# Decay load on 32 partitions, score operands padded to 128 rows, and fewer fill steps in two batches of an attention and mixer kernel

## The chip, the cores and the metric

The kernel runs on one core of one Trainium2 chip. The metric is the device time in microseconds (us), the median of several executions. A profile's *span* (first to last instruction of one profiled execution) is about 1.8 us shorter than that execution's time in the two main profiles; I compare spans with spans and times with times. The engines are PE (tensor engine; PEld is its weight load), DVE (VectorE), ACT (ScalarE), POOL (GpSimd) and SP (SyncE, which issues transfers).

## The reference

```python
# q, k, v: (8 batches, 8 heads, 576, 64); s: (8, 8, 576)
scores = scale * q @ k.T                       # scale = 1/8
cum    = cumsum(max(s, 0))                     # along the sequence
bias   = min(-(cum[:, None] - cum[None, :]), 0)
attn   = softmax(where(causal, -1e9, scores + bias))
x      = (attn @ v) with the heads side by side     # (8, 576, 512)
u      = x + (x.T @ U @ V).T                   # low rank, along the sequence
out    = u + max(u @ w_ch1, 0) @ w_ch2         # 512 -> 2048 -> 512
```

## The kernel before

Attention and the mixer run interleaved on PE. Attention works on 32 pairs of heads, four pairs a batch. The mixer works on nine groups of 512 tokens, 32 *fill steps* a group (16 of `w_ch1`, 16 of `w_ch2`, four matmuls of 512 columns each). A string of tokens fixes the order: `D`/`E` are score products of a head (diagonal blocks, blocks below), `d f m l` their exponentials on ACT, `A` the product with v, `a` its division on DVE, `U X Y` the low-rank part, `T` a PE transpose of q and k (batches 0 and 1), `G` their transpose on DVE (later batches), `R` the fetch of decay rows, `L` the later decays, `Z` fills, `p` warming matmuls without use, `F` one fill step, `r` what follows it on ACT or DVE.

```python
def load_decays(i, s_sb):                # 32 rows of s, four times over: 128 partitions
    nc.sync.dma_start(out=s_sb, in_=bass.AP(..., i * FR * S, [[0, 4], [S, FR], [1, S]]))

def decays(rows, s_sb, cum):
    blk = [ds(i * FR, FR) for i in range(4)]                 # FR = 32
    nc.vector.tensor_scalar(s_sb, s_sb, 0.0, 1.0 / scale, op0=ALU.max, op1=ALU.mult)
    nc.vector.tensor_tensor_scan(cum, s_sb, s_sb, 0.0, op0=ALU.add, op1=ALU.max)
    nc.scalar.mul(rows[blk[3], 0, :], cum[blk[3]], -1.0)
    nc.scalar.copy(rows[blk[0], 1, :], upper(cum)[blk[0]])
    ...                                                      # two more pieces on DVE

def product(h, dst, j, lo, hi, start, stop):
    bias = bias_0 if h < 2 else None
    rows = D if bias else KA             # 64, or 64 + 4 rows of decays = 68
    nc.tensor.matmul(dst, lhsT=head_of(h)[0:rows, ds(S + j * 128, 128)],
                     rhs=head_of(h)[0:rows, lo:hi], ...)
    if bias:                             # heads 0 and 1: decays as a second product
        nc.tensor.matmul(dst, lhsT=bias[0][:, ds(j * 128, 128)], rhs=bias[1 + h][:, lo:hi], ...)

def play(tokens, pair=None):             # cut
    ...
        if kind == "G":
            n = pair // 2 + i            # group of four heads whose q and k are turned
    ...
            if kind == "y" and n % PB == PB - 1:       # a batch is done: queue its mixer group
                queue(n // PB)
                queue(100 + n // PB)

SEQ = ("p8 T0 tA0 tV0 T1 tA1 tV1 p8 | Z0 D0 d0 T2 tV2 tV2 E0 f0 m0 D1 d1 T3 tV3 tV3 E1 ... "
       "... Y7 yV7 Q1 Q101 F r F r F r F r F r F r F r L1 ")
PAIR = ("D0 d0 U-2 uV-2 X-2 F r E0 k0 f0 G1 m0 F r D1 d1 Y-2 yV-2 F r E1 k1 f1 G1 m1 l0 F r "
        "A-2 K0 a-2 F r A-1 a-1 F r F r F r ")     # from batch 2 on, once a pair
```

The softmax here doesn't subtract the row's maximum and nothing guards it: scores larger than these inputs give would overflow.

## Time and profile before

| | before |
|---|---|
| time, first three runs | 411.49 us (410.84 to 414.21) |
| span of the profile | 410.0 us |
| PE busy | 388.7 us, 95% |
| first score product | 13.98 us |
| first mixer matmul | 45.74 us |
| half clock | 17.17 to 34.24 and 140.05 to 146.88 us |

PE is the bottleneck, so what counts is where it waits and where its clock is low. From the profile's page: the busy table, then the span in 40 slices of 10.25 us; a digit is the busy share, or the granted PE clock, in tenths (9 is 90% or more).

```profile
PE 388.7 (95%) x3358; PEld 222.5 (54%) x3358; DVE 208.2 (51%) x439; ACT 199.1 (49%) x386; POOL 107.4 (26%) x173
...
PE   5999888989999799999999999999999999999996
...
PEclk9858999999999889999999999999999999999999
```

Three places stand out: the first slice is half idle; in slices 2 and 3 PE is "busy" but the clock is at 0.8 and 0.5; at slice 13 PE is at 0.7 and right after it the clock drops again. (The clock records begin with the first change, here at 13.76 us; the time before it is counted as full, though the warming matmuls there start 427 ns apart, which is half clock. The rows "half clock" of my tables begin with the first record too.)

The start, in the chain of waits in order of time (start us, us, what):

```profile
0.80 7.26 DMA hT<-in_s_dram
8.06 0.02 issue
8.09 0.47 DVE hT L185
...
8.58 1.37 DVE hT L186
...
12.11 0.99 DVE hT L601 x2
...
13.13 0.81 DVE slot L220
...
13.98 0.23 PE pscore L250
```

The load of s takes until 8.06 us, the decay operations another 5 us, and only then can DVE copy the first q and k for the first score product.

The hole near slice 13, in PE's timeline (start us, us, engine, line, operation, out<-in; in brackets idle time before it and what ended it):

```profile
133.80 0.81 PE L431 MATMUL pwork<-w_sb,hT 128*128 128x512 bf16 x3
...
137.42 0.42 PE L250 MATMUL pscore<-slot 68*128 68x128 bf16 x5
140.30 0.69 PE L359 MATMUL pwork<-x_sb,U_sb 128*128 128x128 bf16 x5 [2.46 <-DVE x_sb L345]
...
143.10 1.89 PE L414 MATMUL pwork<-uT,w_sb 128*128 128x512 bf16 x4
```

L431 and L414 are the two mixer products. Between 134.5 and 143.10 us there is none, PE waits 2.46 us for a division on DVE, and the four mixer matmuls at 143.10 then take 1.89 us.

### The profile page before, as it was taken

The page shows a single profiled execution, that of the slowest core. Times are in us where ns is not written, and L with a number is a line of the kernel's source. Part 1 is how long each engine was busy: PE and PEld are TensorE (multiplying, and loading weights), DVE is VectorE, ACT ScalarE, POOL GpSimd, SP SyncE. Part 2 cuts the span into 40 slices and gives each one's busy share as a digit, 9 for nine tenths or more (in the row PEclk, how much of TensorE's full clock was granted, in tenths as well). Part 3 has the DMA queues.
Part 4 walks back from the last instruction along what each step waited for, and adds up shares of the span by engine and source line. Part 5 has one row for each costly group of instructions (what it writes and reads, how often), then busy time and mean ns, then how long its engine had stood idle before and what let it go on. Part 6 is the DMA issues. An engine that isn't in the chain of part 4 may idle for free.

```text
span 410.0 us, 8377 instructions
## 1 busy us (share of the span) xinstructions
PE 388.7 (95%) x3358; PEld 222.5 (54%) x3358; DVE 208.2 (51%) x439; ACT 199.1 (49%) x386; POOL 107.4 (26%) x173
## 2 busy tenths in 40 slices
PE   5999888989999799999999999999999999999996
PEld 2367545645555555565556555555555555444442
DVE  4647654578466745665566556655665333102011
ACT  1466487406843557436743674367436730630610
POOL 8871458144304440624052406200000000000000
PEclk9858999999999889999999999999999999999999
DMA  8999999359454961696269625921222001001002
GB/s 124 178 201 154 179 106 127 43 96 212 76 92 92 158 100 30 106 149 108 41 103 153 104 44 96 159 60 32 58 82 57 2 26 53 26 27 55 23 26 77
DMA packets 76294, 37.23 MB, mean 91 GB/s; under 512 B 60616, under 2 KB 67816, under 8 KB 76256
## 3 DMA queue, kind: packets, MB, share of 16 engines
q0 software_dynamic: 65584, 18.43, 51.5%
q1 hardware_dynamic: 10672, 18.28, 15.6%
q8 instruction: 26, 0.43, 0.5%
q14 instruction: 12, 0.10, 0.1%
HBM read 37.95 MB, written 10.03 MB: 117 GB/s over the span
## 4 chain that ended last, share of the span: by engine, by line
PE 85%; DVE 8%; DMA 3%; ACT 2%; POOL 1%; issue 1%; DVEq 0%
PE pwork L414 29%; PE pwork L431 28%; PE pscore L250 11%; PE pwork L329 6%; PE pwork L359 2%; PE pwork L443 2%; DMA hT<-in_s_dram 2%; PE pwork L377 2%; DVE turned L234 2%; PE pwork L397 1%; DVE o_sb L454 1%; DVE uT L404 1%; DVE x_sb L345 1%; PE pscore L259 1%; PE pwork L208 1%; DMA v_slot<-in_v_dram 1%
## 5 line engine op out<-in xcount | busy, mean ns | idle before, releaser
L315 ACT ACTIVATE pT<-pscore 128x512 bf16<-128x512 f32 (+1 forms) x224 | 112.4, 558 | 85.9 <-PE pscore L250 74.2
L414 PE MATMUL pwork<-uT,w_sb 128*128 128x512 bf16 x576 | 140.8, 382 | 1.3 <-DVE uT L404 1.3
L431 PE MATMUL pwork<-w_sb,hT 128*128 128x512 bf16 x576 | 140.4, 379 | 0.0
L421 ACT ACTIVATE hT<-pwork 128x512 bf16<-128x512 f32 x144 | 86.4, 602 | 74.8 <-PE pwork L414 74.0
L414 PEld LDWEIGHTS <-w_sb 128*128 128x128 bf16 x576 | 52.4, 98 | 52.1 <-issue 2.1
L431 PEld LDWEIGHTS <-hT 128*128 128x128 bf16 x576 | 51.7, 98 | 47.9
L250 PE MATMUL pscore<-slot 68*128 68x128 bf16 (+5 forms) x576 | 72.6, 250 | 2.8 <-ACT pT L315 1.9
L250 PEld LDWEIGHTS <-slot 68*128 68x128 bf16 (+1 forms) x576 | 45.2, 101 | 37.6 <-issue 8.5
L454 DVE COPY o_sb<-pwork 128x512 f32<-128x512 f32 x36 | 24.9, 692 | 70.9 <-PE pwork L443 70.9
L126 POOL DMA_DIRECT2D qk_sd<-in_q_dram x48 | 27.1, 575 | 125.6 <-DVE turned L234 109.1
L234 DVE STREAM_TRANSPOSE turned<-qk_sd 128x576 bf16<-128x576 bf16 x48 | 54.5, 1138 | 0.7
L329 PEld LDWEIGHTS <-pT 128*128 128x128 bf16 x960 | 38.3, 99 | 14.5 <-issue 2.0
L318 DVE TENSOR_TENSOR pT<-pT,keep 128x512 bf16<-128x512 bf16 (+1 forms) x84 | 29.8, 355 | 28.2 <-ACT pT L315 27.3
L329 PE MATMUL pwork<-v_slot,pT 128*128 128x65 bf16 x960 | 40.6, 196 | 1.5 <-ACT slot L220 1.2
L370 DVE CAST ux<-pwork 128x128 bf16<-128x128 f32 x30 | 8.7, 290 | 48.1 <-PE pwork L359 48.1
L345 DVE TENSOR_TENSOR x_sb<-pwork,rec 128x320 bf16<-128x320 f32 x64 | 31.5, 492 | 2.2
L126 POOL DMA_DIRECT2D qk_sd<-in_k_dram x48 | 27.1, 573 | 9.1 <-DMA w_sb<-in_moe_w_ch_dram 7.3
L134 POOL DMA_DIRECT2D v_slot<-in_v_dram x32 | 28.5, 902 | 0.5 <-DMA uT<-in_q_dram 0.5
L404 DVE CAST uT<-pwork 128x512 bf16<-128x512 f32 x30 | 20.5, 684 | 14.2 <-PE pwork L397 14.2
L220 DVE COPY slot<-pwork 64x576 bf16<-64x576 bf16 x25 | 19.8, 797 | 9.3 <-PE pwork L208 9.0
L344 DVE RECIPROCAL rec<-pwork 128x5 f32<-128x5 f32 x64 | 12.2, 191 | 18.6 <-PE pwork L329 18.4
L359 PE MATMUL pwork<-x_sb,U_sb 128*128 128x128 bf16 x160 | 14.5, 222 | 5.6 <-DVE x_sb L345 5.6
(75 smaller groups left out, 177.5 us busy)
## 6 DMA issues: line engine op xcount, KB each, us to landing
out_dram<-o_sb SPq DMA_DIRECT2D x36, 256.0 KB
slot<-turned SPq DMA_DIRECT2D x96, 72.0 KB
w_sb<-in_moe_w_ch_dram POOLq DMA_DIRECT2D x8, 512.0 KB, 13.3
v_slot<-in_v_dram POOLq DMA_DIRECT2D x32, 128.0 KB, 5.9
qk_sd<-in_q_dram POOLq DMA_DIRECT2D x48, 72.0 KB, 3.6
qk_sd<-in_k_dram POOLq DMA_DIRECT2D x48, 72.0 KB, 4.2
uT<-in_q_dram POOLq DMA_DIRECT2D x2, 288.0 KB, 9.8
uT<-in_k_dram POOLq DMA_DIRECT2D x2, 288.0 KB, 10.0
```

The source lines that it names most:

```text
L126: nc.gpsimd.dma_start(out=qk_t[g][ds(32 * a, 32), c, :].rearrange("p (n f) -> p n f", n=6), in_=src[g // 2, 4 * (g % 2) + a].rearrange("(n ...
L134: nc.gpsimd.dma_start(out=vt[:, t, :, 0:D], in_=v[b, :, ds(t * 128, 128), :].rearrange("h p d -> p h d"),)
L234: nc.vector.transpose(turned[:, e, c].rearrange("p (n m t) -> p n t m", n=6, t=3), src[:, c].rearrange("p (n t e d) -> p e n t d", n=6, t= ...
L250: nc.tensor.matmul(dst, lhsT=head_of(h)[0:rows, ds(S + j * 128, 128)], rhs=head_of(h)[0:rows, lo:hi], start=start, stop=stop and not bias, ...
L315: nc.scalar.activation(dst, src, EXP, scale=scale)
L318: nc.vector.tensor_tensor(p, p, m, op=ALU.min)
L329: nc.tensor.matmul(po[:, i, :], lhsT=p_of(h)[:, ds(spot(j, i), 128)], rhs=v_slots[h // H % 3][:, j, h % H, :], start=(j == 0), stop=(j == ...
L345: nc.vector.tensor_tensor(x_of[b][:, :, ds(h % H * D, D)], po[:, :, 0:D], rec.to_broadcast([128, 5, D]), op=ALU.mult,)
L414: nc.tensor.matmul(f1, lhsT=w1_sb[nf // 4][:, kt, ds(nf % 4 * 128, 128)], rhs=uT[:, kt, ds(g * 512, 512)], start=(kt == 0), stop=(kt == 3),)
L421: pending.append(lambda nf=nf, f1=f1: nc.scalar.activation(hT[:, nf, :], f1, RELU))
L431: nc.tensor.matmul(f2, lhsT=hT[:, nf, ds(i * 128, 128)], rhs=w2_sb[nf // 4][:, nf % 4, :], start=(nf == 0), stop=False, skip_group_check=True,
L454: nc.vector.tensor_copy(o_sb, f2)
```

## The change

Three things. The decays are loaded once, on 32 partitions, and the pieces are written from there. From head 2 on the score products contract over all 128 rows (rows 68 to 127 are zero), for which the slots are zeroed at the start. In batches 2 and 3 two of the eight fill steps of each pair are left out, so that the queue of mixer work lasts longer, and from batch 2 on q and k are turned half a pair sooner. Smaller parts go with these: the first head is loaded alone, 10 and 4 warming matmuls stand where 8 and 8 stood, and the later decays are worked out one operation at a time between fill steps. Cut to its core:

```diff
     def load_decays(i, s_sb):
         nc.sync.dma_start(out=s_sb,
-            in_=bass.AP(..., i * FR * S, [[0, 4], [S, FR], [1, S]]))
+            in_=s.rearrange("b h s -> (b h) s")[ds(i * FR, FR)])
@@ decays: also a "yield" after each operation
-        nc.scalar.mul(rows[blk[3], 0, :], cum[blk[3]], -1.0)
+        nc.scalar.mul(rows[blk[3], 0, :], cum, -1.0)
@@ product
-        rows = D if bias else KA
+        rows = D if bias else 128
@@ play
+            if kind == "e":                 # a fill step from batch 4 on only
+                if pair >= 4 * PB:
+                    feed()
+                continue
-                    n = pair // 2 + i
+                    n = (pair + 1) // 2 + i
@@ opening
-        load_first(0, 2)
+        load_first(0, 1)
         make_identity(nc, identity)
+        load_first(1, 1)
...
+        nc.vector.memset(slots[0][D:, 0:2, 2 * S :], 0.0)
+        clear(slots[0][D:, 2:4, :])         # on ScalarE
+        clear(slots[1][D:, :, :])
@@ the two fills of v_slots[0] moved behind the decays
@@ SEQ
-        "p8 T0 tA0 tV0 T1 tA1 tV1 p8 | Z0 D0 ...
+        "p10 T0 tA0 tV0 T1 tA1 tV1 p4 | Z0 Z1 R2 Z2 D0 ...
-        ... Q1 Q101 F r F r F r F r F r F r F r L1 "
+        ... Q1 Q101 R5 F r L F r L F r L F r G5 F r L F r G5 F r L L L L "
@@ PAIR
-        "A-2 K0 a-2 F r A-1 a-1 F r F r F r "
+        "A-2 K0 a-2 e r A-1 a-1 F r F r e r "
```

## The prediction

> **What bounds it now.** The tensor engine (PE): 388.7 of 410.0 us busy (engine table), 85% of the chain of waits. Losses:
>
> 1. *Start.* The first score product begins at 13.98 us. The chain in order of time: decay load 0.80 to 8.06 us, the decay operations on VectorE 8.09 to 13.10, one copy, PE. That load uses only four of the sixteen DMA engines, which then delay the first q and k: twelve report the first q by 5.9 us, those four at 8.3 to 8.45.
> 2. *Half clock, opening.* The clock records show 0.5 from 17.2 to 34.2 us, and there the chain is PE without a gap.
> 3. *Filler runs out.* From 135 to 142 us (timeline) no mixer matmuls are interleaved; PE waits 2.46 us for a VectorE result, streams for about 27% of the 3.4 us before 140.0, and is then granted 0.5 from 140.0 to 146.9 us.
>
> [...] the two half-clock stretches last 17.07 and 6.83 us, five and two windows. I weighted streaming time per window by rows/128. The clock fell after 0.35 and 0.24, did not fall at 0.40; it did not rise after windows at half clock that streamed 99% of the time with weighted 0.70 to 0.75, and rose after 0.83 and 0.89. So, my inference, rows count, and padding 68 rows to 128 should let the clock rise earlier. It costs PE nothing: after a 448-column product of 68 rows the next starts 193 ns later, the rate of the 128-row mixer matmuls (215 ns for 512).
>
> **What the change does.**
> - Decays on 32 partitions: a quarter of the bytes, spread over all engines as the 32-partition transposed blocks are (about 1.9 us from issue to landing). Landing about 3.3 us. VectorE then needs the same 5.0 us, starting near 3.8 (it waits for the identity). First head loaded alone: first q, k about 5.3 us. First score product near 10.2 us: **-3.8 us**, on the chain.
> - Padding: zeroing adds about 3.3 us on ScalarE before 6 us (idle there) and about 4 us on VectorE after the first copies, which has slack. Heads 0 and 1 still use 64 rows, so I expect half clock until about 5 us after head 2 (10 us before): **-1.5 us** net, since the 3.4 us of full clock at 13.8 us may be lost.
> - Fewer fill steps: about 32 steps are left at batch 2; at six a pair they last until the next group is ready. Work only moves later. Removes 2.8 us of lost streaming and 3.4 us of half clock; **-5.6 us** after some small new waits.
> - Turning sooner, later decays spread: about 0.
>
> **Prediction:** 411.5 - 10.9 = **400.6 us**, range 396 to 405. Faster by over 2% 0.80, within 2% 0.19, slower 0.01.
>
> **Right if:** first score product at 9.5 to 11 us; decay load landed before 4.5 us; no half clock near 140 us and no mixer-free stretch; opening half clock ends before 29 us; first mixer matmul at about 40.5 us (now 45.8).
>
> **Wrong if:** the clock phase or the lower activity at the start keeps half clock as long as before (then about 402.5); the VectorE zeroing delays heads 2 and 3; six-fill pairs leave PE waiting for VectorE (about 6 of 8.6 us busy) and give back some of step 3.

The windows of 3.4 us are those of the clock records of the kernel before: each whole stretch there is a multiple of 3.413 us (3.413, 17.067, 105.813, 6.827). 3.8, 1.5 and 5.6 us make the 10.9. Its times of the zeroing were my estimates; in the changed kernel it took 3.32 us on ScalarE (from 2.09 us) and 3.32 us on VectorE (12.37 us on, with a small piece at 11.66).

## The result and the profile after

| | before | after |
|---|---|---|
| time, 4 runs each | 411.83 us (410.84 to 414.21) | 399.95 us (398.62 to 400.64) |
| ratio | | 0.970 (0.9648 to 0.9751) |
| span | 410.0 us | 397.5 us |
| first score product | 13.98 us | 10.65 us |
| head 2 begins | 23.98 us | 22.25 us |
| first mixer matmul | 45.74 us | 42.06 us |
| head 16 (batch 2) begins | 94.06 us | 90.37 us |
| half clock | 17.17 to 34.24, 140.05 to 146.88 | 9.42 to 26.48 |

A ratio is the mean time of one kernel's fast runs over that of the other's of the same rounds, so not quite the ratio of the medians.

The page after:

```profile
PE 377.4 (95%) x3300; PEld 218.5 (55%) x3356; DVE 209.2 (53%) x443; ACT 202.6 (51%) x388; POOL 108.2 (27%) x175
...
PE   6998788989999999999999999999999999999996
...
PEclk9569999999999999999999999999999999999999
```

A slice is now 9.94 us. The dip at slice 13 and the clock loss behind it are gone; the half clock of the opening is there, only earlier. (Some matmul records are missing, 3300 against 3356 weight loads, so PE's busy time is slightly low.)

The chain in order of time, after, first 11 us:

```profile
3.48 0.37 DVE hT L182
...
3.88 1.36 DVE hT L184
...
7.28 1.64 DVE hT L621 x2
...
9.01 0.10 DVE v_slot L624
...
9.27 0.49 DVE v_slot L625
...
9.80 0.81 DVE slot L224
...
10.65 0.28 PE pscore L254
```

The load has left the chain: all sixteen engines had reported it by 2.62 us, and the decays start when DVE has the identity. The first score product comes 3.33 us sooner. Two new pieces stand in the chain: the fills of `v_slot` (0.79 us from 9.01 us to the copy, with the gaps), which the change moved there, and the two scalings at L621, 1.64 us against 0.99 before.

PE's timeline, after, at about the same heads as the hole above (L435 and L418 are the mixer products now):

```profile
126.74 0.81 PE L435 MATMUL pwork<-w_sb,hT 128*128 128x512 bf16 x3
127.39 1.08 PE L333 MATMUL pwork<-v_slot,pT 128*128 128x65 bf16 x30
128.30 1.02 PE L435 MATMUL pwork<-w_sb,hT 128*128 128x512 bf16 x4
129.16 0.39 PE L447 MATMUL pwork<-identity,uT 128*128 128x128 bf16 x4
129.39 1.03 PE L435 MATMUL pwork<-w_sb,hT 128*128 128x512 bf16 x4
130.25 0.42 PE L254 MATMUL pscore<-slot 128*128 128x128 bf16 x5
```

Mixer matmuls stand between the attention's without a break.

Where the 12.5 us of span came from, with the start of a head's first weight load as the mark (the same work lies between the same marks, except that fill steps moved):

| stretch | before | after | gained |
|---|---|---|---|
| start to head 0 | 13.98 | 10.65 | 3.33 |
| head 0 to head 2 | 10.00 | 11.60 | -1.60 |
| head 2 to first mixer matmul | 21.76 | 19.81 | 1.95 |
| first mixer matmul to head 16 | 48.32 | 48.31 | 0.01 |
| head 16 to the end | 315.97 | 307.14 | 8.83 |

Of the last row, heads 32 to 62 alone, where both kernels run 120 fill steps, gained 1.42 us (154.61 to 153.19).

### The profile page after: what moved, and what is told of

It is laid out like the page before. It is cut to its first block, busy times and chain, and to the rows that moved or that the text cites. A ratio compares the mean times of both kernels' runs of the same rounds, so it can differ in the third digit from the quotient of the medians.

```text
span 397.5 us, 8329 instructions
## 1 busy us (share of the span) xinstructions
PE 377.4 (95%) x3300; PEld 218.5 (55%) x3356; DVE 209.2 (53%) x443; ACT 202.6 (51%) x388; POOL 108.2 (27%) x175
## 4 chain that ended last, share of the span: by engine, by line
PE 89%; DVE 5%; ACT 3%; issue 2%; POOL 0%; DVEq 0%; POOLq 0%
PE pwork L435 30%; PE pwork L418 30%; PE pscore L254 11%; PE pwork L333 6%; PE pwork L363 2%; PE pwork L447 2%; PE pwork L401 2%; PE pwork L381 2%; ACT pT L319 1%; PE pscore L263 1%; DVE slot L224 1%; DVE x_sb L349 1%; PE pwork L212 1%; DVE turned L238 1%; ACT slot L224 1%
## 5 line engine op out<-in xcount | busy, mean ns | idle before, releaser
L418 PE MATMUL pwork<-uT,w_sb 128*128 128x512 bf16 x551 | 137.5, 379 | 1.3
L435 PE MATMUL pwork<-w_sb,hT 128*128 128x512 bf16 x548 | 135.8, 379 | 1.5
L435 PEld LDWEIGHTS <-hT 128*128 128x128 bf16 x576 | 52.3, 98 | 50.3
L418 PEld LDWEIGHTS <-w_sb 128*128 128x128 bf16 x576 | 52.1, 98 | 49.6 <-issue 0.3
L254 PE MATMUL pscore<-slot 128*128 128x128 bf16 (+5 forms) x576 | 71.0, 246 | 5.9 <-DVE slot L224 3.4
L254 PEld LDWEIGHTS <-slot 128*128 128x128 bf16 (+1 forms) x576 | 44.2, 99 | 39.1 <-issue 6.1
L333 PEld LDWEIGHTS <-pT 128*128 128x128 bf16 x960 | 36.0, 98 | 11.3 <-issue 1.5
L333 PE MATMUL pwork<-v_slot,pT 128*128 128x65 bf16 x960 | 38.5, 193 | 1.5 <-ACT slot L224 1.2
L408 DVE CAST uT<-pwork 128x512 bf16<-128x512 f32 x30 | 20.5, 683 | 18.0 <-PE pwork L401 18.0
```

Source lines behind the costliest of these rows:

```text
L333: nc.tensor.matmul(po[:, i, :], lhsT=p_of(h)[:, ds(spot(j, i), 128)], rhs=v_slots[h // H % 3][:, j, h % H, :], start=(j == 0), stop=(j == ...
L418: nc.tensor.matmul(f1, lhsT=w1_sb[nf // 4][:, kt, ds(nf % 4 * 128, 128)], rhs=uT[:, kt, ds(g * 512, 512)], start=(kt == 0), stop=(kt == 3),)
L435: nc.tensor.matmul(f2, lhsT=hT[:, nf, ds(i * 128, 128)], rhs=w2_sb[nf // 4][:, nf % 4, :], start=(nf == 0), stop=False, skip_group_check=True,
```

## The experiments

Twelve kernels ran, all gave correct results. A group's kernels ran on one chip together; the groups ran on different chips. Only group 1 has the changed kernel on its own chip; totals of groups 2 and 3 are set against it through the ratio to the kernel before, or by profiles. Besides times I compare profiles by the marks above and by the clock records.

How the "row-weighted activity" of my expectations is worked out: for each 3.413 us window that the clock records mark off, the time that matmuls stream their columns (2.4 columns per ns, or 1.2 at half clock, worked out from the starts of 512-column matmuls, 215 and 427 ns apart), each weighted by its rows over 128, divided by the window. It is a model, and missing records make it a little low. In the two main profiles (the time before their first records taken at half clock, as the starts 427 ns apart show) the clock rose after windows of 0.77, 0.83 to 0.84 and 0.89 (before) and twice 0.96 (after), and did not rise after windows of 0.75 or less; it fell after 0.35 to 0.36 and 0.24 (before), after 0.30 (after) and at the idle end, and stayed full after 0.40 and more. In the first of these, before the fall at 17.17 us, no gap was over 1 us. These are figures of two profiles, not a threshold; in other profiles I noted exceptions.

### Group 1: undoing one part of the change at a time

**e1_control**: the changed kernel again.

> The changed kernel again, unaltered, as the control of this group. All theories: 399 to 401 us, first score product near 10.7 us, a half-clock stretch of about five windows (17 us) in the opening whose start may shift by up to one window of 3.4 us, none near 140 us.

Measured: 399.31 us (398.7 to 399.48), first score product 10.65 us, half clock 9.07 to 26.14 us, none near 140 us. As expected.

**e1_k68**: padding undone.

```diff
-        rows = D if bias else 128
+        rows = D if bias else KA
```

> The changed kernel, but with score products of 68 rows again (the zeroing stays). Theory (rows count for the clock): from head 2 on the row-weighted activity stays near 0.70 until the value products come, so the opening half clock lasts about two windows longer (near 24 us instead of 17) and the first mixer matmul comes about 2 us later; total 2 to 2.5 us above the control, nothing after 45 us changes. Rival A (only streaming time counts, padding does nothing): same as control within 0.5 us, same half clock. Rival B (padding speeds each product at full clock too): the stretch from head 32 to head 62 also becomes longer, 1 us or more.

Measured: 402.18 us (401.36 to 403.08), 2.9 us above the control; the span is 1.95 us above. (Its six runs fell into two groups, near 401.4 us with a mean clock of 0.974 and near 403.0 us with 0.968; the profile is of the first, so the 2 us below are those of the faster group.) Half clock lasted 20.5 us, 11.59 to 32.07. By luck the clock's windows stood at the same phase as in e1_fill8 below (11.60 us), whose opening is that of the changed kernel, so those two compare best. Busy times by stretch (stretch, its length, PE, PEld, DVE, ACT and POOL busy time, granted clock, DMA share, GB/s), e1_k68:

```profile
21.80:25.20 3.40, 3.40 (x28) 2.50 (x26) 2.37 (x3) 2.25 (x5) 2.20 (x4) 0.50 1.40 184
25.20:32.00 6.80, 6.80 (x76) 5.54 (x74) 3.61 (x8) 5.36 (x10) 6.16 (x10) 0.50 1.28 210
```

and e1_fill8, padded:

```profile
21.80:25.20 3.40, 3.40 (x28) 2.51 (x27) 2.35 (x3) 2.27 (x5) 2.17 (x4) 0.50 1.38 182
25.20:32.00 6.80, 5.84 (x114) 4.96 (x113) 4.99 (x12) 6.51 (x13) 6.21 (x10) 1.00 1.28 211
```

In the first stretch both do the same work with PE busy throughout; the row-weighted activity was 0.70 with 68 rows and 0.96 with 128. Then the padded one has full clock and issues 114 matmuls where the other issues 76; the 68-row one had to wait two windows more. The first mixer matmul came at 43.63 us against 41.59. Rival A fell. Heads 32 to 62 took 153.40 us against 153.19: rival B is worth 0.2 us at most. Padding acts through the clock, in the opening, and is worth about 2 us there.

**e1_fill8**: eight fill steps a pair again in batches 2 and 3.

```diff
             if kind == "e":
-                if pair >= 4 * PB:
-                    feed()
+                feed()
                 continue
```

> The changed kernel, but with eight fill steps a pair in batches 2 and 3 again. Theory: the mixer steps run out before pair 13, a stretch of about 7 us without mixer matmuls comes back near 130 us and with it two windows (6.8 us) of half clock; 6 to 8.5 us above the control. Rival (padding and the earlier turning alone keep the clock up there, or the gap was due to late turned q and k): the mixer-free stretch comes back but without half clock, at most 3 us above the control.

Measured: 406.28 us (406.19 to 407.53), 7.0 us above the control. The mixer-free stretch is back (the last mixer matmuls of the old group start at 130.87 us, the first of the next at 140.14), with the same wait:

```profile
137.59 0.45 PE L363 MATMUL pwork<-x_sb,U_sb 128*128 128x128 bf16 x5 [2.47 <-DVE x_sb L349]
```

Half clock followed for one window, 137.90 to 141.31 us, not two. The next window reached 0.87 in row-weighted activity, where the kernel before had reached only 0.75 and had to wait for another, so in these two profiles padding shortens this clock loss too but doesn't prevent it. From head 16 to the end it took 313.94 us, 6.79 more than the control. (Before head 16 it was 1.22 us later than the control: its clock fell for one window at 62.80 us; see the end of this section.) The theory holds, the rival falls.

This run also shows where heads 32 to 62 gained. They took 154.42 us here, near the 154.61 of before. PE's waits for the copy of a finished batch into `uT`, in us in total, times, and the longest, in before:

```profile
PE pwork L414 <- DVE uT L404: 1.3, 5, 0.5
```

and in e1_fill8:

```profile
PE pwork L418 <- DVE uT L408: 1.3, 5, 0.5
```

In the changed kernel and in e1_k68 no such wait exists. Four of the five, 0.2 us each, lie in heads 32 to 62; the longest, 0.46 us, comes after head 62. So they are 0.8 us of the 1.23 us that these heads lost here against the control; the rest stands in no wait of PE's matmuls that the profile lists. With eight fill steps from batch 2 on the queue runs empty just as each batch is ready, and the first step of the next group waits for the copy made a moment before. The steps left over by the change (at head 32, 79 done instead of 86) stay in the queue as a reserve for the rest of the kernel.

**e1_gpair**: q and k turned as late as before (the fetch of a group's decay rows moves with it).

```diff
-                    n = (pair + 1) // 2 + i
+                    n = pair // 2 + i
-        ... Q1 Q101 R5 F r L F r L F r L F r G5 F r L F r G5 F r L L L L "
+        ... Q1 Q101 F r L F r L F r L F r F r L F r F r L L L L "
```

> The changed kernel, but q and k turned as late as before (half a pair later). Theory (turning sooner was worth about 0): within 0.5 us of the control. Rival (the 1.4 us that heads 32 to 62 gained came from q and k being ready sooner): those heads take 1 to 1.5 us longer again, total 1 to 2 us above the control.

Measured: 401.01 us (399.69 to 401.35), 1.7 us above the control; the span is 1.0 us above. All of the span's difference arose between head 18 and head 32; heads 32 to 62 took 153.17 us. So my "0" was wrong, and the rival named the wrong heads. A wait that the control has not:

```profile
PEld L254 <- DMA slot<-turned: 1.5, 2, 0.8
```

Where a pair has only six fill steps it is short, and q and k turned in the pair just ahead land too late. With eight steps nothing shows. Turning sooner is what keeps the six-step pairs from this wait.

### Group 2: the load, and what the clock counts

**e2_load4**: the decays on 128 partitions again, in one transfer.

```diff
-            in_=s.rearrange("b h s -> (b h) s")[ds(i * FR, FR)],
+            in_=bass.AP(..., i * FR * S, [[0, 4], [S, FR], [1, S]]),
```

(and the pieces taken from their own blocks, as before)

> The changed kernel, but the decays loaded four times over on 128 partitions as before, in one transfer. Theory (the load was late because it went over only four DMA engines, and those four then also delayed the first q and k): it lands near 8 us again, some engines report the first q near 7.5 to 8.5 us, the first score product comes at 13.5 to 14.5 us, and the total is 3 to 4 us above the changed kernel, 402 to 404 us.

Measured: 403.93 us (402.1 to 404.84), first score product 14.46 us. The load's four reports came at 7.22 to 7.70 us; twelve engines reported the first q by 4.59 us, four between 7.4 and 7.9. As expected. The first product is 0.48 us later than in the kernel before, so what else the change did in the opening gained nothing there.

A caution for reading: the profile gives this run a mean clock of 0.998, and 1.00 in every slice of the opening, yet the products of head 2 start 107 ns apart, which is half clock for 128 columns (at full clock they start 56 ns apart). Its clock records begin only at the first change, at 31.10 us; the time before is counted as full.

**e2_load16**: the same bytes, as four transfers of 32 rows.

```diff
-        nc.sync.dma_start(out=s_sb, in_=s.rearrange(...)[ds(i * FR, FR)])
+        for a in range(4):
+            nc.sync.dma_start(out=s_sb[ds(a * FR, FR)], in_=s.rearrange(...)[ds(i * FR, FR)])
```

> The changed kernel, but the decays loaded on 128 partitions with four transfers of 32 rows each: the same bytes as before, in 32-row pieces. Theory (the number of engines used was the cause, not the bytes): every piece is spread over all engines, the last lands at 4.5 to 5.5 us, first score product at 11 to 12 us, total at most 1.5 us above the changed kernel. Rival (the fourfold bytes were the cause): lands after 7 us, first score product after 13 us, 3 to 4 us above.

Measured: 402.23 us (401.1 to 402.72); first score product 12.14 us, 0.14 us past what I had expected. DVE's timeline shows when the decays could start; here, and then in e2_load4:

```profile
5.01 0.59 DVE L183 TENSOR_SCALAR hT<-hT 128x576 f32<-128x576 f32 x1 [1.54 <-DMA hT<-in_s_dram]
```

```profile
7.73 0.46 DVE L186 TENSOR_SCALAR hT<-hT 128x576 f32<-128x576 f32 x1 [4.25 <-DMA hT<-in_s_dram]
```

The same bytes in four transfers of 32 rows come 2.72 us sooner: that is the larger part of what the narrow load gained (3.40 us is where the changed kernel starts them, held by the identity), and the bytes and the extra issues are the smaller part. The total missed my bound of 1.5 us above (it is 2.3 above the first measurement of the changed kernel, on another chip); in the profiled run 1.7 of 3.1 us arose when the clock fell for one window at 64.45 us.

What the traces show of the engines: the transfer with `[[0, 4], ...]` was reported by four (7.82 to 8.06 us in the kernel before, 7.22 to 7.70 in e2_load4), the one of 32 rows by sixteen (2.43 to 2.62 us in the changed kernel). What sets that number was not tested.

**e2_spin64** and **e2_spin128**: what does the clock count? The 10 warming matmuls become 20, of 64 or of 128 rows.

```diff
-            nc.tensor.matmul(idle[0], lhsT=warm[:, 0:128], rhs=warm, start=True, stop=True)
+            nc.tensor.matmul(idle[0], lhsT=warm[0:64, 0:128], rhs=warm[0:64], start=True, stop=True)
-        "p10 T0 ...
+        "p20 T0 ...
```

> The changed kernel with 20 warming matmuls in place of 10, each of 64 rows (same 512 columns, same time). A test of what the clock counts, beside the next run. Theory (rows count): the activity of their windows is 0.5, so the clock does not rise while they run; their starts stay 427 ns apart to the last. Rival (only streaming time counts): the clock rises within two windows, at the latest near 7.4 us, and the later ones start 215 ns apart.

> The same with 20 warming matmuls of 128 rows. Both theories: the clock rises before 7.5 us and the later ones start 215 ns apart.

PE's timeline of e2_spin64, then of e2_spin128:

```profile
1.29 8.71 PE L498 MATMUL pwork<-warm 64*128 64x512 bf16 x20 [1.29 <-DVE warm L105]
```

```profile
1.29 6.52 PE L498 MATMUL pwork<-warm 128*128 128x512 bf16 x20 [1.29 <-DVE warm L105]
```

Same columns, same count. With 64 rows all twenty stay 427 ns apart. With 128 rows the starts are 427 ns apart up to 5.1 us and 216 ns from 5.5 us on. One single run each (403.03 and 398.64 us), but the contrast lies within each trace. So here the rows decided: 8.7 us of streaming with 64 rows did not raise the clock, and with 128 rows it rose after about 4 us. That rows count was an inference in the prediction and is shown here.

### Group 3: looking for a faster version

In the changed kernel the opening stays at half clock until head 2. Heads 0 and 1 alternate a 64-row product and a 128-row one, and these start 218 and 222 ns apart for 128 columns, though 107 ns would do at half clock. In e3_pad01 heads 0 and 1 are padded as well.

```diff
-        rows = D if bias else 128
+        rows = 128
-        nc.vector.memset(slots[0][D:, 0:2, 2 * S :], 0.0)
-        clear(slots[0][D:, 2:4, :])
-        clear(slots[1][D:, :, :])
+        clear(slots[0][D:, :, :])
@@ behind the decays
+        clear(slots[1][D:, :, :])
@@ SEQ: "Z2" taken out
```

> The changed kernel, but heads 0 and 1 padded to 128 rows as well (their rows zeroed first, on ScalarE, slot 1 cleared after the decays; the later zeroing on VectorE falls away). Theory: in the changed kernel each product of these two heads (64 rows) and the bias product after it (128 rows) follow each other 107 ns later than their columns need at half clock, because the row count changes each time and the weight load is not hidden; 36 such products cost about 3.9 us. With one row count this goes: 2.9 to 4 us less from the first product to head 2 (11.6 us now), and the fuller windows let the clock rise earlier. First score product within 0.5 us of the changed kernel, first mixer matmul 4 to 6 us sooner, total 4 to 6 us below it. Rival (the gaps come from two products adding to the same output, not from the row count): head 2 comes at the same distance from the first product, within 1 us; total within 1.5 us.

PE's timeline of the changed kernel, then of e3_pad01:

```profile
11.09 0.29 PE L254 MATMUL pscore<-slot 64*128 64x128 bf16 x1
11.31 0.29 PE L263 MATMUL pscore<-hT 128*128 128x128 bf16 x1
11.53 0.29 PE L254 MATMUL pscore<-slot 64*128 64x128 bf16 x1
```

```profile
10.89 0.31 PE L254 MATMUL pscore<-slot 128*128 128x128 bf16 x1
11.00 0.31 PE L263 MATMUL pscore<-hT 128*128 128x128 bf16 x1
11.11 0.31 PE L254 MATMUL pscore<-slot 128*128 128x128 bf16 x1
```

The row count is the cause: 107 ns at the same half clock, with the same two products adding to the same output, so the rival falls. The weight loads show it as well: in the changed kernel the load for the product at 11.31 us starts at 11.30 us, in e3_pad01 the one for 11.00 us at 10.89 us, a product ahead. At full clock too: 158 to 162 ns alternating (before, from 13.98 us), 56 ns with one row count (after). Why a change of row count costs this is not shown. From head 0 to head 2 it took 5.64 us instead of 11.60. But the time is 399.65 us (398.57 to 400.94): nothing was gained.

**e3_spin16** (`p16` in place of the second `p4`), **e3_pad01spin** (both) and **e3_all** (both, and the fills of `v_slot` moved to where DVE waits for the identity):

> The changed kernel with 16 warming matmuls in place of 4 after the second transposes, so that the tensor engine is busy until the first score product. Theory (full clock was spent on waiting): half clock begins one window later, at about 12.5 us or later, and the stretch from the first product to head 2 (11.6 us) gets 0.5 to 1.7 us shorter, as the 64-row heads let the clock fall anyway; total 0.5 to 1.5 us below the changed kernel.

> Both: heads 0 and 1 padded, and 16 warming matmuls. Theory: the clock is full when the first product starts and the padded heads hold it there, so there is no half clock in the opening, or one of at most two windows; first product to head 2 about 5 us, first mixer matmul at 33 to 37 us, total 6 to 8 us below the changed kernel (392 to 394 us). If the opening is then bound by ScalarE or the loads instead, the gain over padding alone is under 1 us.

> The same, and the two fills of v_slot, which stand in the chain just before the copy for the first score product, moved to where VectorE waits for the identity. Theory: first score product 0.6 to 0.8 us sooner, and the total with it: 391.3 to 393.4 us.

| kernel | time | ratio to before | head 0 | head 2 | head 6 | first mixer matmul | half clock |
|---|---|---|---|---|---|---|---|
| after (e1_control) | 399.31 | 0.9655 | 10.65 | 22.25 | 32.00 | 42.04 | 9.1 to 26.1 |
| e3_pad01 | 399.65 | 0.9699 | 10.64 | 16.28 | 32.02 | 42.25 | 10.9 to 14.3, 24.5 to 31.3, 41.6 to 45.0 |
| e3_spin16 | 398.32 | 0.9663 | 10.65 | 21.08 | 30.20 | 40.26 | 13.0 to 23.3 |
| e3_pad01spin | 399.14 | 0.9684 | 10.64 | 16.14 | 30.83 | 41.07 | 23.3 to 30.1, 40.4 to 43.8 |
| e3_all | 399.62 | 0.9686 | 10.68 | 16.18 | 31.46 | 41.70 | 23.9 to 30.7, 41.0 to 44.4 |

With padding the kernels reach head 4 at 19.4 to 19.5 us instead of 26.7, and by head 6 have lost all of it or all but 0.5 to 1.2 us. PE's timeline of e3_pad01spin shows the new wall:

```profile
20.62 0.25 PE L333 MATMUL pwork<-v_slot,pT 128*128 128x65 bf16 x3 [0.48 <-DMA v_slot<-in_v_dram]
22.40 0.28 PE L333 MATMUL pwork<-v_slot,pT 128*128 128x65 bf16 x4 [1.52 <-DMA v_slot<-in_v_dram]
23.46 0.43 PE L333 MATMUL pwork<-v_slot,pT 128*128 128x65 bf16 x5 [0.78 <-DMA v_slot<-in_v_dram]
24.84 0.22 PE L333 MATMUL pwork<-v_slot,pT 128*128 128x65 bf16 x1 [0.95 <-DMA v_slot<-in_v_dram]
```

PE waits 3.7 us for v of batch 0, which in the order of transfers stands behind the first block of `w_ch1`; behind the window with the first two of these waits (2.00 of its 3.41 us) the clock is at half for two windows (23.3 to 30.1 us), and the gain is gone. This cause is read from the trace; no run loaded v sooner. My expectations of 4 to 8 us missed: I had not looked at when v lands. e3_all missed by its own step as well: DVE was free 0.7 us sooner, but ACT, kept by the later clearing of slot 1, finished its copy at the old time, and DVE's copy waits for that one (0.81 us idle). e3_spin16's half clock began 3.6 us later than after's, as expected, and its span is 1.8 us shorter in one profile; its ratio to before, 0.9663 (0.9635 to 0.9691), lies no lower than the control's 0.9655 (0.9629 to 0.968). So no version here is shown to beat the changed kernel. Loading v ahead of `w_ch1` together with padded heads 0 and 1 is the untried next step.

**Left open.** Why L621's two scalings took 1.64 us in the changed kernel and 0.65 us in e2_load4 was not tested. The clock's extra drop near 62 to 65 us (in e1_fill8, e2_load16 and e2_spin64) followed windows of 0.35 to 0.36 activity; in the changed kernel, whose windows stood at another phase, the lowest there was 0.44. The windows' phase differs from run to run (the fall in the opening came at 9.42 us in the first profile of the changed kernel, at 9.07 in e1_control). Some of the scatter between runs may come from that; I argued it from profiles only.

## Why the prediction was right or wrong

The time was predicted at 400.6 us and measured at 399.95; the range held it, and the sign and the size of the gain (10.9 predicted, 11.9 between the medians) were right. Three of the four terms, however, were off, and partly cancelled; that the sum came so close is partly luck.

1. *Start, -3.8 us predicted; 3.33 measured. Right.* Undoing it (e2_load4) put the first product back to 14.46 us. The load came even sooner than predicted (2.62 against 3.3 us). What I missed is that the fills of `v_slot` had moved into the chain, and that the two scalings got slower. The cause, a transfer over four engines, is shown by e2_load16 for most of it (2.72 us).
2. *Padding, -1.5 us net predicted; -0.35 measured (21.76 to 19.81, less 10.00 to 11.60). Right in mechanism, mis-sized.* The step named "may be lost" was lost in full: the clock was full from 6.00 to 9.42 us, while PE waited for DVE, and half all through heads 0 and 1, which cost 1.60 us (e3_spin16, whose clock stayed full until 13.01 us, took 10.43 us for these heads instead of 11.60). The gain after head 2 was 1.95 us. The clock rose 4.2 us after head 2 began, against "about 5". e1_k68 (0.70 with 68 rows, 0.96 with 128) and the warming pair (427 ns to the last, or 216 from 5.5 us on) show that rows count.
3. *Fewer fill steps, -5.6 us predicted; 8.83 measured from head 16 on. Right in mechanism, too small.* e1_fill8 gives back 6.79 of it, which is the figure shown for the fill steps alone. The other 2 us were there already in e1_fill8: 1.60 of them in heads 18 to 32 (68.71 us before, 67.11 in e1_fill8), where e1_fill8, which keeps the padding, lost one window of clock and the kernel before two. The sum had credited all of that to the fill steps. I had allowed for small new waits and found instead that old ones went: with the reserve of steps heads 32 to 62 gained 1.23 us, 0.8 of it in the wait at the end of each batch, which my sum did not contain.
4. *Turning sooner, "about 0". Wrong in size.* e1_gpair shows about 1 us of span. I judged it by itself; it matters because pairs with six fill steps are shorter.
5. *Wrong if:* the zeroing on DVE did not delay head 2 (PE was busy without a gap from 10.65 to 22.25 us); six-step pairs did not leave PE waiting.

The signs to look for held: first product at 10.65 us, load before 4.5 us, no half clock near 140 us, opening half clock over before 29 us. The first mixer matmul came at 42.06 us, 1.6 us later than "about 40.5", the sum of the misses in 1 and 2.

## What to carry to other kernels

When filler work hides the latencies of another stage, ration it so that it lasts until the next portion is ready and a little stays over: here that was worth more than everything done at the start. Here low clock came after a window of idle or thin PE work (0.24 before the 6.83 us of half clock from 140.05 us), so look at the rows of small matmuls as well as at gaps; and alternating products of 64 and of 128 rows took 218 to 222 ns a product instead of 107 at half clock, 158 to 162 instead of 56 at full clock. (68 rows next to 128 did no such harm: heads 32 to 62 took 153.40 us in e1_k68 against 153.19.) And look for the next wall before sizing a gain: halving the time of two heads gained nothing here, because PE then waited for v.
